# A newly searched order for the first 235 operations of an attention and feed-forward kernel

## The chip, the core and the metric

The kernel runs on one core of a Trainium2 chip. The core has a matrix engine (TensorE, PE in the tables), a vector engine (VectorE, DVE), a scalar engine (ScalarE, ACT), a general engine (GpSimd, POOL) and a queue engine (SyncE, SP) that issues most transfers. Each of them executes its own list of instructions strictly in the order in which the program holds them, and waits at an instruction until what it needs is there. The metric is the device time of one execution in microseconds (us); lower is better.

## The reference, cut to what matters

```python
scores = scale * q_c @ k_c.T                  # 8 x 8 heads, 576 positions in chunks of 64, depth 64
attn = softmax(scores)                        # exp(s - max) / (sum + 1e-9)
x = (attn @ v_c)                              # becomes 4608 rows x 512
h = x @ w_in                                  # 512 x 2048
g = h - tanh(h)
out = g @ w_out                               # 2048 x 512
```

## The kernel before

The 4608 rows are 36 pairs of chunks of 128 rows each, and four pairs make a group of 512 rows; there are nine groups. The first group is the start of the program and is special in two ways. Its weights arrive as 64-bit words and have to be turned into two fp32 halves (high and low) on ScalarE and VectorE first, and its products are fp32 products; the groups after it use fp16 halves. So the first group runs beside the attention of pairs 0 to 7, the loading of all weights and their conversion, and nobody but a hand-searched table, `PLAN`, says in which order this work stands.

`PLAN` is a string of tokens. The program walks through it from left to right and issues the token's instructions, each on the engine that it belongs to; what remains of the order is one list per engine. The tokens that the text below speaks of:

| token | engine | what it does (line) |
|---|---|---|
| `a3`, `v3`, `l1.0`, `l1.1` | SP | load q and k of pair 3; its v; w_in (`.0`) and w_out (`.1`) of block 1 into one of three raw buffers |
| `F9` | PE | nine products of a zero tile `warm`, result in the bank `idle`, read by nobody (L793) |
| `S3`, `T3`, `V3` | PE | scores of pair 3 (L182), its transposed weights (L173), its weighted values (L182) |
| `m3`, `b0`, `r3`, `N3`, `Y3` | DVE | row maximum (L214), subtraction (L219), reciprocals (L240, L241), normalising (L245), low half of x (L275) |
| `E3`, `e0`, `t3`, `X3` | ACT | exponents with the sums in eight parts (L236) or in one (L223), copies out of PSUM (L258), high half of x (L271) |
| `A1`, `H1.0` | ACT | magnitude of weight block 1 (L144), its high half (L159) |
| `s1`, `o1`, `O1`, `L1.0` | DVE | shift (L148), low bits (L152), sign (L156), low half (L163) |
| `G1.1`, `G3` | PE | first feed-forward product of block 1 for rows 256 to 511 (`.0`: rows 0 to 255), of block 3 for all 512 rows (L557) |
| `i1.1`, `k1.1` / `j1.1`, `q1.1` | ACT / DVE | tanh (L568) and high half (L584) / subtraction (L575) and low half (L592) of the same piece |
| `P1.1` | PE | second feed-forward product of that piece (L602) |
| `W1.1` | POOL | a transfer that adds a weight's low half to its high half (L813) |

A product `G` writes a PSUM bank of the pool `ps_h`, which has two. The bank is free for the next product once `j` of the same piece has read it. The zero products write a bank of the same pool, taken once, ahead of the plan:

```python
ps_h = ctx.enter_context(tc.tile_pool(name="ps_h", bufs=2, space=PSUM))
idle = ps_h.tile([P, MOST], F32, name="ph")
    elif kind == "F":
        for _ in range(n):
            nc.tensor.matmul(idle, lhsT=warm[:, :P], rhs=warm, start=True, stop=True)
def gemm1(self, fc, t0, t1):
    ph = ps_h.tile([P, MOST], F32, name="ph")[:, :n]
```

Before, the last `F` token stands ahead of the first `G`, so from the first product on both banks take turns: G1.1, G0.1, G0.0, G3, G1.0 use bank 1, 0, 1, 0, 1 in that order. The attention of pairs 0 to 3 uses two further bank pairs in turn (`two_banks`), where the next pair's step waits until the reader of the pair before is done.

Of the kernel before, what the change touches and what calls it, by code (L numbers as in the profile page):

```python
# [48 lines left out]


PLAN = """
a3 l0.0 a0 a1 l1.0 l1.1 a2 v0 v3 F9 S3 l0.1 l3.0 m3 a5 A0.0 v2 B3 v1 E3 s0.0 l3.1 o0.0 F7 S0 O0.0 a7 m0 H0.0 F3 S1 r3 b0 a4 m1 e0 N3 b1 A1 L0.0 F8 T3 e1 s1 S2 t3 z1 a6 m2 F2 V3 r1 B2 o1 E2 v6 N1 O1 X3 r2 A0.1 l6.0 Y3 l6.1 H1.1 N2 F13 T1 J1.1 s0.1 T2 z0 t1 o0.1 t2 F1 V1 r0 O0.1 V2 X1 v5 N0 H0.1 l8.0 Y1 v4 X2 l8.1 J0.1 L0.1 F4 S5 Y2 H1.0 m5 A3 F1 T0 L1.0 t0 B5 s3 F2 G1.1 E5 o3 V0 O3 G0.1 v7 X0 i1.1 Y0 H3.0 l9.1 S7 l9.0 j1.1 i0.1 L3.0 H3.1 G0.0 k1.1 j0.1 L3.1 k0.1 m7 G3 A6 q0.1 B7 q1.1 i0.0 s6 E7 j0.0 o6 G1.0 L1.1 i3 O6 S6 i1.0 A9 y P1.1 j3 l5.1 l5.0 H6.0 m6 P0.1 H6.1 s9 J6.0 L6.0 k3 B6 o9 G6 W0.6 E6 q3 O9 k0.0 S4 L6.1 J1.0 W0.1 l7.0 l7.1 q0.0 P3 H9.0 m4 H9.1 j1.0 A5 B4 L9.1 L9.0 E4 s5 G9 r7 o5 k1.0 N7 A7 q1.0 O5 T7 i9 P1.0 W1.1 t7 s7 l10.0 H5.1 l10.1 j9 P0.0 W1.0 H5.0 L5.1 k9 L5.0 J5.0 V7 o7 G5 W0.5 X7 q9 O7 A10 r6 l4.1 Y7 P9 l4.0 N6 H7.0 i5 s10 H7.1 L7.0 J5.1 j5 T6 o10 k5 G7 t6 q5 i6 O10 j6 l2.0 H10.1 P5 W1.5 l2.1 L7.1 i7 r5 J10.1 j7 k6 L10.1 A8 q6 V6 N5 k7 P6 s8 H10.0 X6 q7 J10.0 L10.0 Y6 J6.1 W1.6 o8 A2 T5 P7 t5 O8 J3.0 W0.3 s2 H8.0 l15.0 l15.1 H8.1 o2 J8.0 V5 J8.1 G10 L8.0 O2 X5 L8.1 H2.0 l13.0 Y5 l13.1 A4 G8 L2.0 r4 J2.0 s4 i10 N4 J3.1 W1.3 j10 J9.1 W1.9 T4 o4 G2 i8 t4 O4 k10 H2.1 q10 l12.1 H4.1 l12.0 j8 J2.1 V4 L2.1 k8 P10 J4.1 q8 A13 L4.1 i2 s13 H4.0 P8 j2 J7.1 o13 J4.0 J9.0 W0.9 L4.0 O13 k2 G4 A15 q2 l14.0 X4 l14.1 s15 Y4 Wx o15 P2 Z H13.0 i4 L13.0 H13.1 j4 J0.0 W0.0 L13.1 J13.1 G13 O15 k4 A14 q4 l11.1 l11.0 H15.0 s14 H15.1 L15.0 P4 J15.0 L15.1 J15.1 o14 i13 A12 j13 G15 O14 k13 J13.0 s12 H14.0 q13 H14.1 o12 J14.0 P13 J14.1 L14.0 i15 L14.1 J7.0 j15 A11 O12 G14 k15 s11 H12.1 q15 H12.0 L12.1 J12.1 L12.0 P15 J12.0 o11 i14 j14 O11 k14 G12 q14 H11.1 H11.0 L11.1 J11.1 L11.0 J11.0
"""
# [937 lines left out]
```

## Time and profile before

| | us |
|---|---|
| median of three runs (lowest, highest) | 799.54 (799.11, 799.78) |
| the profiled execution | 799.48 |
| its span in the trace | 797.7 |
| TensorE busy in the span | 789.5 (99%) |
| VectorE, ScalarE busy | 628.4 (79%), 496.1 (62%) |
| TensorE busy in the first 10 us, from 10 to 25.3 | 8.49, 13.10 |

The profiled execution lies 0.06 us below the median and 1.8 us above its own span. In the span VectorE is nearly always busy from 10 us on until 77 us (15.16 of 15.30 us between 10 and 25.3), TensorE from 25.3 us on until the end. Rows of the trace read: start, duration, engine, line, operation, output tile <- input tiles, sizes, count, and in brackets how long the engine had been idle and what released it. Consecutive instructions of an engine overlap a little, so the difference between two starts is what an instruction adds to a busy engine.

### The profile page before, as it was taken

The page shows a single profiled execution, that of the slowest core. Times are in us where ns is not written, and L with a number is a line of the kernel's source. Part 1 is how long each engine was busy: PE and PEld are TensorE (multiplying, and loading weights), DVE is VectorE, ACT ScalarE, POOL GpSimd, SP SyncE. Part 2 cuts the span into 40 slices and gives each one's busy share as a digit, 9 for nine tenths or more (in the row PEclk, how much of TensorE's full clock was granted, in tenths as well). Part 3 has the DMA queues.
Part 4 walks back from the last instruction along what each step waited for, and adds up shares of the span by engine and source line. Part 5 has one row for each costly group of instructions (what it writes and reads, how often), then busy time and mean ns, then how long its engine had stood idle before and what let it go on. Part 6 is the DMA issues. An engine that isn't in the chain of part 4 may idle for free.

```text
span 797.7 us, 16317 instructions
## 1 busy us (share of the span) xinstructions
PE 789.5 (99%) x6650; PEld 521.8 (65%) x6650; DVE 628.4 (79%) x1134; ACT 496.1 (62%) x958; POOL 46.5 (6%) x82
## 2 busy tenths in 40 slices
PE   8999999999999999999999999999999999999998
PEld 4777884445676666666666666666666666666664
DVE  7999999999999997868777777777776777655443
ACT  6989968986675656556655555566555655454333
POOL 0022135500000000000000000000000000000000
PEclk9999999999999999999999999999999999999999
DMA  9888848853131223111312231203211220001001
GB/s 359 307 230 227 222 130 177 146 133 80 40 107 40 81 63 110 53 50 46 106 54 53 54 95 50 62 22 97 63 54 42 67 67 15 14 1 53 1 1 54
DMA packets 58731, 72.36 MB, mean 91 GB/s; under 512 B 32800, under 2 KB 33056, under 8 KB 58528
## 3 DMA queue, kind: packets, MB, share of 16 engines
q1 hardware_dynamic: 53760, 61.75, 24.8%
q0 software_dynamic: 4752, 9.44, 6.9%
q8 instruction: 52, 0.85, 0.4%
q14 instruction: 23, 0.19, 0.1%
q10 hardware_dynamic: 144, 0.13, 0.0%
HBM read 45.09 MB, written 9.44 MB: 68 GB/s over the span
## 4 chain that ended last, share of the span: by engine, by line
PE 87%; DVE 8%; ACT 2%; DMA 1%; issue 1%; SPq 0%; DVEq 0%; ACTq 0%
PE po L715 35%; PE ph L657 22%; PE psa L657 9%; PE ph L557 8%; PE po L602 7%; PE psa L423 2%; PE psa L182 2%; DVE w L152 1%; DMA raw<-w_out 1%; PE ps L182 1%; DVE w L156 1%; PE ph L793 1%; DVE wl L163 1%; DMA out<-t 0%; DVE w L148 0%
## 5 line engine op out<-in xcount | busy, mean ns | idle before, releaser
L715 PE MATMUL po<-wl,gh 128*128 128x512 f16 x672 | 154.2, 379 | 0.0
L715 PE MATMUL po<-wl,gl 128*128 128x512 f16 x672 | 154.2, 379 | 0.0
L657 PEld LDWEIGHTS <-wh 128*128 128x128 f16 x1344 | 128.0, 98 | 24.1 <-issue 0.4
L657 PE MATMUL ph<-xh,wl 128*128 128x256 f16 x672 | 114.6, 273 | 0.0
L715 PEld LDWEIGHTS <-gl 128*128 128x128 f16 x672 | 65.8, 98 | 68.0
L715 PEld LDWEIGHTS <-gh 128*128 128x128 f16 x672 | 65.8, 98 | 67.5
L657 PEld LDWEIGHTS <-wl 128*128 128x128 f16 x1008 | 98.6, 98 | 17.2
L657 PE MATMUL ph<-xl,wl 128*128 128x256 f16 x336 | 91.6, 273 | 0.0
L657 PE MATMUL ph<-xh,wh 128*128 128x256 f16 x448 | 76.7, 273 | 0.0
L657 PE MATMUL psa<-xh,wh 128*128 128x256 f16 x448 | 76.4, 273 | 0.3 <-ACT m L649 0.3
L602 PE MATMUL po<-wl,gh 128*128 128x512 f16 (+1 forms) x192 | 63.2, 383 | 0.0
L657 PE MATMUL psa<-xl,wh 128*128 128x256 f16 x224 | 61.1, 273 | 0.0
L657 PE MATMUL ph<-xl,wh 128*128 128x256 f16 x224 | 61.1, 273 | 0.0
L379 ACT ACTIVATE s<-s 128x512 f32<-128x512 f32 x24 | 15.1, 629 | 56.6 <-DVE s L370 56.6
L683 ACT ACTIVATE t<-t,sig 128x512 f32<-128x512 f32 x37 | 26.7, 721 | 35.2 <-DVE t L679 35.0
L683 ACT ACTIVATE t<-wh,sig 128x512 f32<-128x512 f32 x38 | 27.4, 721 | 33.5 <-DVE wh L679 33.3
L683 ACT ACTIVATE t<-spare,sig 128x512 f32<-128x512 f32 x37 | 26.7, 721 | 33.5 <-DVE spare L679 33.5
L557 PE MATMUL ph<-xl,wl 128*128 128x512 f16 x192 | 43.8, 379 | 0.2 <-DVE t L573 0.2
L679 DVE TENSOR_TENSOR t<-ph,t 128x512 f32<-128x512 f32 x28 | 19.2, 686 | 21.9 <-PE ph L657 21.3
L679 DVE TENSOR_TENSOR wh<-ph,wh 128x512 f32<-128x512 f32 x28 | 19.2, 686 | 20.1 <-PE ph L657 19.4
L436 DVE TENSOR_TENSOR xl<-wh,xh 128x512 f16<-128x512 f32 (+1 forms) x56 | 34.3, 615 | 0.4 <-ACT xh L436 0.2
L687 DVE SCALAR_TENSOR_TENSOR wh<-wh,sig,t 128x512 f32<-128x512 f32 x38 | 28.4, 748 | 7.8 <-ACT t L683 7.6
(173 smaller groups left out, 1485.8 us busy)
## 6 DMA issues: line engine op xcount, KB each, us to landing
raw<-w_in SPq DMA_DIRECT2D x16, 512.0 KB, 6.4
raw<-w_out SPq DMA_DIRECT2D x16, 512.0 KB, 6.4
wh<-wl POOLq DMA_DIRECT2D x32, 256.0 KB, 4.2
rawv<-vL SPq DMA_DIRECT2D x28, 256.0 KB, 2.7
rawq<-qL SPq DMA_DIRECT2D x28, 256.0 KB, 3.0
rawk<-kL SPq DMA_DIRECT2D x28, 256.0 KB, 3.2
out<-wh SPq DMA_DIRECT2D x28, 256.0 KB, 2.0
qk<-qkE SPq DMA_DIRECT2D x8, 512.0 KB, 8.7
```

Of the source, the lines that this page charges most:

```text
L152: nc.vector.scalar_tensor_tensor(out=w, in0=low, scalar=29, in1=w, op0=ALU.logical_shift_right, op1=ALU.bitwise_or)
L182: nc.tensor.matmul(ps[os, r, hp * CH:(hp + 1) * CH], lhsT=lhsT(rs, hp, o), rhs=rhs(rs, hp, o), start=True, stop=True)
L379: nc.scalar.activation(s, s, AF.Exp, scale=scale)
L423: nc.tensor.matmul(ps[:, hp, c, :], lhsT=self.v16[p % len(self.v16)][a][:, c, hp, :], rhs=d["a16"][:, b, hp, cs], start=(k == 0), stop=(k ...
L436: return (lambda: nc.scalar.copy(out=h, in_=a)), (lambda: nc.vector.tensor_sub(l, a, h))
L557: nc.tensor.matmul(ph, lhsT=self.weight(fc, 0, a)[:, kc * P:(kc + 1) * P], rhs=x[b][:, kc, cols], start=(k == 0), stop=(k == 3 * KC - 1))
L602: nc.tensor.matmul(self.po[t], lhsT=gg[a][:, ts], rhs=self.weight(fc, 1, b), start=(k == 0), stop=(k == 3 * FC - 1))
L657: nc.tensor.matmul(bank[:, q * 2 * P:(q + 1) * 2 * P], lhsT=self.weight(u, a, i, q, kc), rhs=self.x[j][:, b, kc, :], start=(first and q == ...
L679: nc.vector.tensor_tensor(out=c, in0=self.banks["X"], in1=self.m5 if n % 4 == 3 else c, op=ALU.subtract if n % 4 == 2 else ALU.add)
L683: nc.scalar.activation(t, self.now[n][0], AF.Tanh, scale=self.ff.sig)
L687: nc.vector.scalar_tensor_tensor(out=c, in0=c, scalar=self.ff.sig, in1=t, op0=ALU.mult, op1=ALU.subtract)
L715: nc.tensor.matmul(ff.po[t], lhsT=g[a][:, ts], rhs=half_w[1][fc][:, b], start=(first and s == 0 and k == 0), stop=(last and s == 1 and k = ...
```

## The change

The first 235 tokens of `PLAN` are put into another order; the work in them stays the same, save for the zero products, of which there are 41 in ten tokens instead of 50 in ten. The code is not changed. The two versions agree again from the same token on each engine: TensorE from `P5` on, VectorE from `L7.1` on, apart from a few neighbours that swap places further behind without changing any engine's own list.

```diff
@@ PLAN
-a3 l0.0 a0 a1 l1.0 l1.1 a2 v0 v3 F9 S3 l0.1 l3.0 m3 a5 A0.0 v2 B3 v1 E3 s0.0 l3.1 o0.0 F7 S0 O0.0 a7
+a3 l0.0 a0 a1 a2 l0.1 v2 l1.0 F6 S3 v3 l1.1 m3 a5 A0.0 v1 B3 E3 s0.0 l3.0 l3.1 o0.0 F5 S0 v0 O0.0 m0
...
-X2 l8.1 J0.1 L0.1 F4 S5 Y2 H1.0 m5 A3 F1 T0 L1.0 t0 B5 s3 F2 G1.1 E5 o3 V0 O3 G0.1 v7 X0 i1.1 Y0 H3.0 l9.1 S7 l9.0 j1.1 i0.1 L3.0 H3.1 G0.0
+V2 o1 X1 X2 Y1 A3 Y2 F3 S5 O1 T0 G0.1 t0 m5 l9.0 H1.0 s3 a6 H1.1 V0 v4 L1.0 i0.1 v5 B5 X0 o3 G1.1 l9.1 E5 a4 v7 j0.1 O3 Y0 k0.1 l7.1 F4 S7 H3.0 L1.1 i1.1 G0.0
...
```

The zero products in order: before 9, 7, 3, 8, 2, 13, 1, 4, 1, 2, all ahead of the first `G`; now 6, 5, 3, 1, 3, 3, 11, 3 ahead of the first `G`, then 4 behind `G1.1` and 2 behind `G0.0`. Two places show what moves.

The first place is VectorE from `Y2` on, the last low half of x that the first feed-forward product needs (`xl`), to the first subtraction out of a product's bank (`t<-ph`). In the names the number behind the underscore only tells tiles apart; `wl01` is the low half of block 1's w_in, `w_364` is block 1's words and `w_435`, before `w_492`, block 3's. Before:

```order
L275 TENSOR_TENSOR xl_117<-ps2_433,xh_116 128x4x128
L214 TENSOR_REDUCE mx_489<-ps2_469 128x8
L163 TENSOR_TENSOR wl01_75<-w_291,wh01_74 128x512
L231 TENSOR_SCALAR mx_489<-mx_489 128x8
L148 TENSOR_SCALAR w_492<-w_492 128x1024
L152 SCALAR_TENSOR_TENSOR w_492<-raw_201,w_492 128x1024
L156 SCALAR_TENSOR_TENSOR w_492<-raw_201,w_492 128x1024
L275 TENSOR_TENSOR xl_117<-ps2_529,xh_116 128x4x128
L575 TENSOR_TENSOR t_563<-ph_507,t_563 128x256
```

And the same place now, from `Y2` to `q0.1` (`gl_547`):

```order
L275 TENSOR_TENSOR xl_117<-ps2_414,xh_116 128x4x128
L156 SCALAR_TENSOR_TENSOR w_364<-raw_170,w_364 128x1024
L214 TENSOR_REDUCE mx_480<-ps2_441 128x8
L148 TENSOR_SCALAR w_435<-w_435 128x1024
L163 TENSOR_TENSOR wl01_75<-w_364,wh01_74 128x512
L231 TENSOR_SCALAR mx_480<-mx_480 128x8
L152 SCALAR_TENSOR_TENSOR w_435<-raw_218,w_435 128x1024
L575 TENSOR_TENSOR t_510<-ph_464,t_510 128x256
L156 SCALAR_TENSOR_TENSOR w_435<-raw_218,w_435 128x1024
L275 TENSOR_TENSOR xl_117<-ps2_490,xh_116 128x4x128
L163 TENSOR_TENSOR wl11_77<-w_364,wh11_76 128x512
L592 TENSOR_TENSOR gl_547<-t_510,gh_546 128x256
```

The sign of block 1 (`O1`, L156 on `w_364`) has moved from ahead of `Y2` to behind it; nothing else has crossed `Y2`. The subtraction `j0.1` (L575 on `ph_464`) stands behind `O1`, `m5`, `s3`, `L1.0`, `B5` and `o3`. The next three rows behind `gl_547` are `m7` (L214), `L3.0` (L163) and `j1.1` (L575 on `ph_517`).

The second place is TensorE from the first feed-forward product on, with the waits that the program holds. Before:

```order
L557 MATMUL ph_507<-xh_116,wh01_74 128x256 [waits Activation_49]
L557 MATMUL ph_507<-xh_116,wh01_74 128x256 x3
L557 MATMUL ph_507<-xh_116,wl01_75 128x256 [waits DVE_49]
L557 MATMUL ph_507<-xh_116,wl01_75 128x256 x3
L557 MATMUL ph_507<-xl_117,wh01_74 128x256 x4
L182 MATMUL ps2_529<-aT_501,v_170 64x64 [waits DMAHW7_49,Activation_49]
L182 MATMUL ps2_529<-aT_501,v_170 64x64 x15
L557 MATMUL ph_547<-xh_116,wh00_70 128x256 [waits PE_49]
```

And now, the same engine from `G0.1` (`ph_464`) over `V0` (L182) to `G1.1` (`ph_517`):

```order
L557 MATMUL ph_464<-xh_116,wh00_70 128x256 [waits Activation_49]
L557 MATMUL ph_464<-xh_116,wh00_70 128x256 x3
L557 MATMUL ph_464<-xh_116,wl00_71 128x256 x4
L557 MATMUL ph_464<-xl_117,wh00_70 128x256 x4
L182 MATMUL ps2_490<-aT_477,v_244 64x64 [waits DMAHW6_49,Activation_49]
L182 MATMUL ps2_490<-aT_477,v_244 64x64 x15
L557 MATMUL ph_517<-xh_116,wh01_74 128x256 [waits DVE_49]
```

Behind it stand four zero products, `S7`, then `G0.0` (`ph_576`, which waits for VectorE too), two zero products and `G1.0` (`ph_605`). Since zero products are still to come, the bank `idle` stays taken until the last of them: G0.1, G1.1 and G0.0 all lie in bank 1 of the two now, and G1.0 is the first to get bank 0. The VectorE instruction that `G1.1` waits for is `j0.1`, and the one that `G0.0` waits for is `j1.1`.

More of the change, by code (lines that the diff above doesn't have):

```diff
@@ L51 @@
 PLAN = """
-a3 l0.0 a0 a1 l1.0 l1.1 a2 v0 v3 F9 S3 l0.1 l3.0 m3 a5 A0.0 v2 B3 v1 E3 s0.0 l3.1 o0.0 F7 S0 O0.0 a7 m0 H0.0 F3 S1 r3 b0 a4 m1 e0 N3 b1 A1 L0.0 F8 T3 e1 s1 S2 t3 z1 a6 m2 F2 V3 r1 B2 o1 E2 v6 N1 O1 X3 r2 A0.1 l6.0 Y3 l6.1 H1.1 N2 F13 T1 J1.1 s0.1 T2 z0 t1 o0.1 t2 F1 V1 r0 O0.1 V2 X1 v5 N0 H0.1 l8.0 Y1 v4 X2 l8.1 J0.1 L0.1 F4 S5 Y2 H1.0 m5 A3 F1 T0 L1.0 t0 B5 s3 F2 G1.1 E5 o3 V0 O3 G0.1 v7 X0 i1.1 Y0 H3.0 l9.1 S7 l9.0 j1.1 i0.1 L3.0 H3.1 G0.0 k1.1 j0.1 L3.1 k0.1 m7 G3 A6 q0.1 B7 q1.1 i0.0 s6 E7 j0.0 o6 G1.0 L1.1 i3 O6 S6 i1.0 A9 y P1.1 j3 l5.1 l5.0 H6.0 m6 P0.1 H6.1 s9 J6.0 L6.0 k3 B6 o9 G6 W0.6 E6 q3 O9 k0.0 S4 L6.1 J1.0 W0.1 l7.0 l7.1 q0.0 P3 H9.0 m4 H9.1 j1.0 A5 B4 L9.1 L9.0 E4 s5 G9 r7 o5 k1.0 N7 A7 q1.0 O5 T7 i9 P1.0 W1.1 t7 s7 l10.0 H5.1 l10.1 j9 P0.0 W1.0 H5.0 L5.1 k9 L5.0 J5.0 V7 o7 G5 W0.5 X7 q9 O7 A10 r6 l4.1 Y7 P9 l4.0 N6 H7.0 i5 s10 H7.1 L7.0 J5.1 j5 T6 o10 k5 G7 t6 q5 i6 O10 j6 l2.0 H10.1 P5 W1.5 l2.1 L7.1 i7 r5 J10.1 j7 k6 L10.1 A8 q6 V6 N5 k7 P6 s8 H10.0 X6 q7 J10.0 L10.0 Y6 J6.1 W1.6 o8 A2 T5 P7 t5 O8 J3.0 W0.3 s2 H8.0 l15.0 l15.1 H8.1 o2 J8.0 V5 J8.1 G10 L8.0 O2 X5 L8.1 H2.0 l13.0 Y5 l13.1 A4 G8 L2.0 r4 J2.0 s4 i10 N4 J3.1 W1.3 j10 J9.1 W1.9 T4 o4 G2 i8 t4 O4 k10 H2.1 q10 l12.1 H4.1 l12.0 j8 J2.1 V4 L2.1 k8 P10 J4.1 q8 A13 L4.1 i2 s13 H4.0 P8 j2 J7.1 o13 J4.0 J9.0 W0.9 L4.0 O13 k2 G4 A15 q2 l14.0 X4 l14.1 s15 Y4 Wx o15 P2 Z H13.0 i4 L13.0 H13.1 j4 J0.0 W0.0 L13.1 J13.1 G13 O15 k4 A14 q4 l11.1 l11.0 H15.0 s14 H15.1 L15.0 P4 J15.0 L15.1 J15.1 o14 i13 A12 j13 G15 O14 k13 J13.0 s12 H14.0 q13 H14.1 o12 J14.0 P13 J14.1 L14.0 i15 L14.1 J7.0 j15 A11 O12 G14 k15 s11 H12.1 q15 H12.0 L12.1 J12.1 L12.0 P15 J12.0 o11 i14 j14 O11 k14 G12 q14 H11.1 H11.0 L11.1 J11.1 L11.0 J11.0
@@ new lines @@
+a3 l0.0 a0 a1 a2 l0.1 v2 l1.0 F6 S3 v3 l1.1 m3 a5 A0.0 v1 B3 E3 s0.0 l3.0 l3.1 o0.0 F5 S0 v0 O0.0 m0 F3 S1 r3 b0 m1 e0 F1 S2 N3 H0.0 b1 z0 e1 F3 T3 m2 A0.1 z1 t3 B2 L0.0 F3 V3 E2 s0.1 r1 o0.1 N1 O0.1 X3 r0 H0.1 l6.0 r2 Y3 l6.1 A1 a7 N2 F11 T1 N0 T2 t1 s1 t2 V1 L0.1 V2 o1 X1 X2 Y1 A3 Y2 F3 S5 O1 T0 G0.1 t0 m5 l9.0 H1.0 s3 a6 H1.1 V0 v4 L1.0 i0.1 v5 B5 X0 o3 G1.1 l9.1 E5 a4 v7 j0.1 O3 Y0 k0.1 l7.1 F4 S7 H3.0 L1.1 i1.1 G0.0 q0.1 H3.1 m7 A6 L3.0 j1.1 i0.0 B7 s6 F2 G1.0 E7 j0.0 o6 y P0.1 L3.1 k1.1 S6 O6 i1.0 A9 G3 m6 l5.1 k0.0 H6.1 s9 l5.0 l7.0 B6 q1.1 E6 q0.0 r7 P0.0 o9 L6.1 H6.0 S4 O9 i3 P1.1 L6.0 H9.0 l10.1 j1.0 l10.0 H9.1 m4 G6 k1.0 A5 j3 N7 k3 B4 L9.0 E4 s5 G9 L9.1 o5 A7 q3 T7 q1.0 O5 i9 P3 j9 H5.0 l8.1 s7 l8.0 H5.1 i6 r6 L5.0 P1.0 J1.1 W1.1 o7 J1.0 W0.1 G5 k9 L5.1 t7 O7 A10 q9 l2.1 J5.0 W0.5 V7 j6 v6 H7.0 s10 P9 J0.1 W1.0 L7.0 i5 o10 k6 X7 j5 H7.1 G7 Y7 k5 O10 J5.1 J6.0 W0.6 N6 l4.0 q5 l4.1 T6 i7 l2.0 L7.1 P5 W1.5 H10.1 r5 j7 A8 L10.1 t6 q6 J10.1 N5 V6 k7 s8 P6 H10.0 q7 X6 L10.0 J10.0 Y6 J6.1 W1.6 o8 A2 T5 P7 O8 t5 J3.0 W0.3 s2 l15.0 H8.0 l15.1 H8.1 o2 V5 J8.0 G10 L8.0 J8.1 O2 X5 L8.1 H2.0 l13.0 Y5 l13.1 A4 G8 L2.0 r4 J2.0 s4 i10 N4 J3.1 W1.3 j10 T4 J9.1 W1.9 o4 G2 i8 t4 O4 k10 H2.1 q10 l12.1 H4.1 V4 j8 l12.0 J2.1 P10 L2.1 k8 J4.1 q8 A13 L4.1 P8 i2 s13 H4.0 j2 J7.1 o13 J4.0 J9.0 W0.9 L4.0 O13 k2 G4 A15 q2 l14.0 X4 l14.1 s15 Y4 Wx P2 o15 Z H13.0 i4 L13.0 H13.1 j4 J0.0 W0.0 L13.1 G13 J13.1 O15 k4 A14 q4 l11.1 l11.0 H15.0 s14 P4 H15.1 L15.0 J15.0 L15.1 J15.1 o14 i13 G15 A12 j13 O14 k13 J13.0 s12 H14.0 q13 H14.1 o12 J14.0 P13 J14.1 L14.0 i15 L14.1 J7.0 j15 G14 A11 O12 k15 s11 H12.1 q15 H12.0 L12.1 J12.1 P15 L12.0 J12.0 o11 i14 j14 G12 O11 k14 q14 H11.1 H11.0 L11.1 J11.1 L11.0 J11.0
```

## The prediction

> **What bounds the kernel now.** I read the stretches first, to see which engine is full where, then the chain of waits, then TensorE's own waits, and last the rows around the moved steps. The columns are busy time (and instructions) of PE, PEld, VectorE, ScalarE and GpSimd, then the granted TensorE clock, the transfer engines' share and GB/s.
>
> ```profile
> 0.00:10.00 10.00, 8.49 (x91) 3.71 (x95) 5.44 (x20) 4.82 (x20) 0.20 (x4) 1.00 0.83 314
> 10.00:25.30 15.30, 13.10 (x238) 7.46 (x238) 15.16 (x32) 12.63 (x35) 0.00 (x0) 1.00 1.03 403
> 25.30:62.00 36.70, 36.67 (x330) 30.32 (x329) 36.53 (x62) 32.87 (x111) 5.82 (x9) 1.00 0.80 243
> 62.00:77.30 15.30, 15.30 (x128) 12.05 (x127) 15.20 (x24) 14.39 (x31) 4.34 (x8) 1.00 0.81 228
> 77.30:133.50 56.20, 56.09 (x276) 41.02 (x275) 52.14 (x90) 45.87 (x90) 18.39 (x32) 1.00 0.73 182
> 133.80:797.70 663.90, 659.75 (x5600) 427.28 (x5599) 503.67 (x910) 385.30 (x674) 17.48 (x32) 1.00 0.23 61
> ```
>
> From 10 to 25.3 us VectorE is the full engine (15.16 of 15.30). From 25.3 us on TensorE is, and stays so: 36.67 of 36.70, 15.30 of 15.30, 56.09 of 56.20. TensorE's waits behind 24 us are three:
>
> ```profile
> PE psa L657 <- ACT m L649: 0.3, 1, 0.3
> PE ps L173 <- DVE xl L275: 0.2, 1, 0.2
> PE ph L557 <- DVE t L573: 0.2, 1, 0.2
> ```
>
> The L173 wait lies ahead of the first feed-forward product; the last row is the wait at 133.8 us, where the fp16 groups have begun. So whatever TensorE loses or wins in the changed stretch arrives at the end, less at most the 0.2 us that it waits there for VectorE anyway. The change is to be judged by one question: when has TensorE done the same feed-forward work? The chain of waits shows that work in order (start, us, engine, tile, line):
>
> ```profile
> 24.59 0.66 PE ps L173 x4
> 25.25 0.43 PE ph L793 x2
> 25.68 1.39 PE ph L557 x12
> 27.07 0.62 PE ps L182 x32
> 27.69 1.57 PE ph L557 x12
> 29.27 0.62 PE ps L182 x32
> 29.92 5.81 PE ph L557 x36
> ```
>
> These are T0, the last two zero products, G1.1, V0, G0.1, S7, then G0.0, G3 and G1.0. At 29.92 us T0, G1.1, G0.1, V0 and S7 are done; the new order has done the same five when it reaches G0.0, since all the attention products ahead of T0 are the same ones. My measure is therefore the start of G0.0, before 29.92 us.
>
> **The change part by part.** First, six zero products instead of nine ahead of S3.
>
> ```profile
> qk<-qkE SPq DMA_DIRECT2D x1, 512.0 KB, 3.7
> 0.74 0.40 SPq L198 DMA_DIRECT2D qk<-qkE  x1
> 1.19 4.02 PE L793 MATMUL ph<-warm 128*128 128x512 bf16 x9 [1.19 <-DVE col L758]
> 5.14 1.13 PE L182 MATMUL ps<-qk 64*64 64x64 f32 x32
> 15.11 2.98 PE L793 MATMUL ph<-warm 128*128 128x512 bf16 x13
> 7.34 2.49 ACT s L236 x16
> 9.85 0.18 DVE sm L240
> 28.18 0.63 ACT L271 CAST xh<-ps 128x512 fp32r<-128x512 f32 x1
> 29.49 0.39 ACT L568 ACTIVATE t<-ph 128x256 f32<-128x256 f32 x1
> ```
>
> The first transfer is issued at 0.74 us and lands 3.7 us later, at 4.44; the scores start at 5.14. They waited for the zero products, not for the data (the wait is booked on the transfer, but landing is 0.7 us older). Nine products take 4.02 us, 0.45 each; six end at 3.9 us. S3 then starts at about 4.5, 0.64 us sooner. Behind it stand m3, then E3 (2.49 us on ScalarE), and the reciprocals r3 at 9.85 us wait for E3: that chain moves along. S0, which VectorE also needs ahead of r3, comes behind five zero products: S3 ends at 5.6; five products are 1.1 us at 0.23 each (2.98/13) and 2.2 at 0.45; S0 at the 1.13 us of a slow S3 ends by 8.9 at worst, so m0 (0.6 us) ends at 9.5 where r3 could start at 9.2. The gain is 0.3 to 0.64 us; I take 0.6, the end that follows if the products behind 6 us run at the later rate.
>
> Second, O1 leaves the stretch ahead of Y2. From 10 us on VectorE has no gap, so Y2 moves by what O1 adds there:
>
> ```profile
> 24.46 0.68 DVE L214 TENSOR_REDUCE mx<-ps 128x8 f32<-128x512 f32 x1
> 25.05 0.68 DVE L163 TENSOR_TENSOR wl<-w,wh 128x512 fp32r<-128x512 f32 x1
> 25.65 0.16 DVE L231 TENSOR_SCALAR mx<-mx 128x8 f32<-128x8 f32 x1
> 25.73 0.68 DVE L148 TENSOR_SCALAR w<-w 128x1024 uint32<-128x1024 uint32 x1
> 26.45 1.23 DVE L152 SCALAR_TENSOR_TENSOR w<-raw,w 128x1024 uint32<-128x1024 uint32 x1
> 27.71 1.23 DVE L156 SCALAR_TENSOR_TENSOR w<-raw,w 128x1024 uint32<-128x1024 uint32 x1
> 28.85 0.68 DVE L275 TENSOR_TENSOR xl<-ps,xh 128x512 fp32r<-128x512 f32 x1
> 29.45 0.41 DVE L575 TENSOR_TENSOR t<-ph,t 128x256 f32<-128x256 f32 x1
> 29.78 0.68 DVE L163 TENSOR_TENSOR wl<-w,wh 128x512 fp32r<-128x512 f32 x1
> ```
>
> By the differences of starts: a maximum 0.59, a low half 0.60, B 0.08, s 0.72, o 1.26, O 1.14, Y 0.60, a half-size j 0.33 (0.41 to its end). O1 is an O: Y2 moves up by 1.14 + 0.6 = 1.74 us. VectorE is free behind Y2 at 24.46 - 1.74 = 22.72, and T0 starts at 24.59 - 1.74 = 22.85.
>
> Third, the bank. TensorE: T0 0.66, G0.1 1.57, V0 0.62, done at 25.7. G1.1 needs the bank of G0.1, so it waits for j0.1. VectorE from 22.72: O1 1.14, m5 0.59, s3 0.72, L1.0 0.60, B5 0.08, o3 1.26, j0.1 to its end 0.41, sum 4.80: 27.5. ScalarE has the tanh i0.1 ready by then: its queue ahead of it holds only t0 and two high halves. G1.1 starts at 27.6; TensorE stood idle for 1.9 us. Behind G1.1 (1.57) come four zero products (0.92) and S7 (0.62): 30.7. VectorE has meanwhile done O3 1.14, Y0 0.60, L1.1 0.60 and q0.1 0.33 (30.1) and waits for S7, because m7 stands ahead of j1.1: m7 0.59, L3.0 0.60, j1.1 0.41 from 30.75 end at 32.35. G0.0 waits for j1.1 and starts at 32.4, after a second idle 1.7 us. That is 2.5 us later than 29.92. Queued behind the waiting G1.1 are S7 and through it E7, s6 and o6; none of them is waited for sooner than TensorE gets there.
>
> Fourth, two zero products behind G0.0, 2 x 0.23 = 0.46 us, on TensorE's path with nothing to cover them: 2.96 us. G1.0 gets the other bank and waits for TensorE alone. Behind it P0.1, S6 and G3 find their inputs. G0.0 ends at 34.0; its tanh (0.39) and E7 (2.49) end near 36.9 us; j0.0 0.33, o6 1.14 and L3.1 0.60 end near 36.6; TensorE wants them at 37.4 and 38.0. From G6 on the banks alternate again. VectorE has waited 0.6 us for S7 and some 1.4 for the tanh of G0.0 by then, so it runs closer to TensorE than before; I bound further waits by 0 and 0.6 us and take 0, the nearest row being 36.67 of 36.70 busy.
>
> Fifth, what I cost at nothing. The transfers are the same ones; w_out of block 1 falls from sixth to tenth place. At 403 GB/s a 512 KB load is 1.3 us, so it lands near 14.9 us, and A1 wants it at 17 or later; if that cover were gone A1 would delay s1 and Y2 by the same. GpSimd's first adds come in another order, W1.1 first instead of W0.6, and start some 12 us later:
>
> ```profile
> 64.63 0.86 POOL L813 DMA_DIRECT2D wh<-wl  x1 [6.88 <-ACT gh L584]
> ```
>
> Before, the queue then idles 6.88 us ahead of W1.5, which waits for work that is later now too; a rest of up to 3 us would hit only later adds, the first readers of which come behind 115 us.
>
> The sum: -1.74 (T0 earlier), -0.43 (two zero products gone ahead of G1.1), +1.9 and +1.7 (two waits for the bank), +1.38 (six zero products among the real ones), +0.15 of rounding and of G halves (1.39 to 1.57) comes to +2.96. Less the 0.2 us wait at 133.8 us that TensorE no longer has: +2.75. Against the profiled execution, 799.48 us (span 797.7, 0.06 below the median), that is 802.2 us.
>
> The Trainium skill, Perfetto Trace Analysis, section Optimizing Tensor Performance, says that independent groups of products should rotate through different PSUM banks, so that reading one out overlaps the next. In the rows above the read-out costs nothing as long as two banks alternate. By the page the change should cost the read-out time between G0.1 and G1.1 and again ahead of G0.0; it gives no figure.
>
> **The rivals.** *No real wait for the bank.* Should G1.1 and G0.0 not wait for j, G1.1 would start with L1.0 at 25.9, S7 would follow E5 (V0 at 25.7, a copy of 0.63 and E5 of 2.49: 28.8) and end at 29.4, and G0.0 would start there: 0.5 us earlier than before, and the two zero products take 0.46 back. That gives 799.4, no change. For it speaks only the table's own order, where G1.1 stands ahead of j0.1; against it the wait that the program holds.
>
> *Faster.* The advance of Y2 would come through whole: 1.74 + 0.43 = 2.17 us, 797.3, if the zero products behind G1.1 and G0.0 only filled waits and j0.1 came before V0's end. It decides at j0.1: VectorE would have to end it by 25.7 instead of 27.5. It has 4.80 us queued behind Y2 and only 2.9 us for it. Waits and zero products together under 0.6 us would make it faster.
>
> *TensorE slow for longer.* The granted clock reads 1.00 throughout, yet the first nine zero products take 0.45 each and the thirteen later 0.23, and the first scores 1.13 us. If with six products, a gap of 0.6 us and S3 the slow rate held until S1, then S0 would end at 8.9, three products at 10.2 and S1 at 11.3, so m1 would start near 11.3 instead of 10.1: 1.2 us more, 803.4 us. The Trainium skill, TensorE: Matmul & The Clock Gate, Part 1, has the array at half rate until a window of about 3.4 us was busy, and back there after as long an idle one. By that rule the waits of 1.9 and 1.7 us would not slow it again; no run here has shown an idle stretch of that length.
>
> **How the numbers follow.** The forecast has 0.62: its own range is 801.2 (the bank waits 1 us shorter, since VectorE's column of 4.8 us is the longest guess) to 803.1 (gain of 0.3 instead of 0.6 at S3, and 0.6 more behind G6). The slow TensorE has 0.12, no wait for the bank 0.16, faster 0.10. About 0.2%, 1.6 us, is what a measurement of this kernel can tell from no change, so slower by more begins at 801.1. Slower is 0.75, the same 0.15, faster 0.10. A range that leaves out the faster case (0.10), the part of the second that ends below 799.5 (0.07) and the third's far end (0.03) reaches from 799.5 to 803.7.
>
> **What would show it.** Right: S3 at about 4.5 us; T0 near 22.9; TensorE idle for about 1.9 us ahead of G1.1 and 1.7 ahead of G0.0, both released by VectorE at L575, G0.0 near 32.4; a full TensorE behind; the wait at 133.8 us gone or put down to a TensorE that is 2.7 us late. Wrong: S3 still at 5.1; no release by L575; products at 0.45 us behind 7 us; or TensorE's lateness at G0.0 absorbed before 133 us, which would need idle time that the rows before do not show.

## The result, and the profile after

| | before | after |
|---|---|---|
| median of six runs each, us (lowest, highest) | 799.49 (799.11, 799.78) | 805.72 (804.34, 807.46) |
| ratio of the two, with its 95% interval | | 1.0079 (1.0069 to 1.0089) |
| the profiled execution, us | 799.48 | 806.50 |
| its span, us | 797.7 | 804.7 |

The change makes the kernel 6.2 us slower; the forecast was 2.7. The stretches of the changed kernel, with the columns and windows of the prediction:

```profile
0.00:10.00 10.00, 7.13 (x110) 3.33 (x111) 6.51 (x23) 4.74 (x20) 0.20 (x4) 1.00 0.81 309
10.00:25.30 15.30, 12.31 (x235) 8.25 (x238) 15.20 (x31) 12.61 (x33) 0.00 (x0) 1.00 0.94 357
25.30:62.00 36.70, 33.46 (x273) 26.22 (x275) 32.58 (x56) 30.02 (x104) 1.93 (x3) 0.95 0.63 219
62.00:77.30 15.30, 15.30 (x129) 12.15 (x128) 13.75 (x20) 12.50 (x28) 7.78 (x10) 1.00 0.90 221
77.30:133.50 56.20, 54.04 (x263) 41.07 (x263) 50.92 (x90) 45.73 (x94) 18.24 (x29) 1.00 0.75 184
```

TensorE was full from 25.3 us on before. Now it misses 3.2 us between 25.3 and 62 us, at a clock of 0.95, and another 2.2 us between 77.3 and 133.5 us. The first hole in TensorE's own rows, from T0 to the product behind the last two zero products:

```profile
22.49 0.66 PE L173 MATMUL ps<-ident,s 128*128 128x128 f32 x4
...
26.94 0.74 PE L557 MATMUL ph<-xh,wh 128*128 128x256 f32 x4 [1.36 <-DVE t L575]
...
31.84 0.93 PE L557 MATMUL ph<-xh,wh 128*128 128x256 f32 x4 [1.75 <-DVE t L575]
32.57 1.06 PE L557 MATMUL ph<-xh,wl 128*128 128x256 f32 x4
33.42 1.05 PE L557 MATMUL ph<-xl,wh 128*128 128x256 f32 x4
34.28 1.08 PE L793 MATMUL ph<-warm 128*128 128x512 bf16 x2
35.42 0.81 PE L557 MATMUL ph<-xh,wh 128*128 128x256 f32 x4
36.06 0.62 PE L557 MATMUL ph<-xh,wl 128*128 128x256 f32 x4
```

The two bracketed rows are G1.1 and G0.0, both released by the subtraction L575. Behind the second wait four products `ph<-xh,wl` take 1.06 us, where they take 0.62 from 36.06 us on, and the granted clock (the last column but two) says why:

```profile
30.00:32.00 2.00, 0.25 (x9) 0.16 (x2) 1.84 (x5) 1.22 (x2) 0.00 (x0) 1.00 1.02 405
32.00:33.00 1.00, 1.00 (x7) 1.00 (x7) 0.46 (x1) 0.00 (x0) 0.00 (x0) 0.61 1.06 420
33.00:34.00 1.00, 1.00 (x6) 1.00 (x6) 0.00 (x0) 0.00 (x0) 0.00 (x0) 0.50 0.65 258
34.00:35.00 1.00, 1.00 (x5) 0.36 (x3) 0.07 (x1) 0.48 (x3) 0.00 (x0) 0.50 0.12 49
```

The second hole lies elsewhere. These are TensorE's waits in it, the first of them at 105.88 us, all ahead of second feed-forward products (L602) for their input (us in total, times, longest):

```profile
PE po L602 <- DVE gl L592: 1.3, 2, 0.8
PE po L602 <- ACT gh L584: 0.9, 1, 0.9
```

They come behind a late load. The chain of waits passes through a late load of w_out in both kernels; before, it stood there as 87.38 with 5.59 us. The changed kernel's:

```profile
92.17 8.01 DMA raw<-w_out
```

ScalarE's magnitude `A` (L144) of that load and of the one ahead of it is my measure of it. First the two rows of before, then those of after:

```profile
86.28 1.16 ACT L144 ACTIVATE w<-raw 128x1024 f32<-128x1024 f32 x1
93.06 1.13 ACT L144 ACTIVATE w<-raw 128x1024 f32<-128x1024 f32 x1 [0.38 <-DMA raw<-w_out]
```

```profile
91.07 1.15 ACT L144 ACTIVATE w<-raw 128x1024 f32<-128x1024 f32 x1
100.28 1.13 ACT L144 ACTIVATE w<-raw 128x1024 f32<-128x1024 f32 x1 [3.39 <-DMA raw<-w_out]
```

The first of the two comes 4.8 us late; from it to the next takes 9.21 us instead of 6.78. I call this the load stretch. ScalarE's lateness is thus 4.8 us by 91 us and 7.2 at 100 us (TensorE's own was 4.2 at T4, which starts at 81.32 instead of 77.11 us); 7.0 reach the end. Beside the load run GpSimd's adds, before and after:

```profile
86.16 0.86 POOL L813 DMA_DIRECT2D wh<-wl  x1 [3.72 <-ACT junk L167]
89.06 0.86 POOL L813 DMA_DIRECT2D xh<-xl  x1 [2.00 <-DVE xl L275]
91.71 0.86 POOL L813 DMA_DIRECT2D wh<-wl  x1 [1.15 <-ACT junk L167]
```

```profile
88.25 0.70 POOL L813 DMA_DIRECT2D wh<-wl  x1
92.56 0.86 POOL L813 DMA_DIRECT2D wh<-wl  x1 [0.18 <-issue]
93.85 0.86 POOL L813 DMA_DIRECT2D xh<-xl  x1 [0.28 <-DVE xl L275]
```

Before, GpSimd waits for data ahead of each of these adds: its queue is empty. After, the brackets are nearly gone: it issues as soon as the add two places earlier has landed (this is waited for by a small copy, `tick`, L812; these waits rise from 28.3 to 41.7 us in all), since the first add comes at 56.5 us instead of 42.7.

So there are three suspects: the held bank, the slow clock, and the adds beside the load.

### The profile page after: what moved, and what is told of

It is laid out like the page before. It is cut to its first block, busy times and chain, and to the rows that moved or that the text cites. A ratio compares the mean times of both kernels' runs of the same rounds, so it can differ in the third digit from the quotient of the medians.

```text
span 804.7 us, 16298 instructions
## 1 busy us (share of the span) xinstructions
PE 789.2 (98%) x6636; PEld 521.4 (65%) x6641; DVE 628.8 (78%) x1134; ACT 496.0 (62%) x958; POOL 49.3 (6%) x82
## 4 chain that ended last, share of the span: by engine, by line
PE 84%; DVE 10%; DMA 3%; ACT 2%; issue 1%; SPq 0%; DVEq 0%; ACTq 0%
PE po L715 35%; PE ph L657 22%; PE psa L657 9%; PE ph L557 6%; PE po L602 6%; PE psa L423 2%; PE psa L182 2%; DMA raw<-w_in 2%; DVE w L152 1%; DVE w L156 1%; DMA raw<-w_out 1%; DVE wl L163 1%; DVE w L148 1%; DVE t L575 1%; ACT w L144 1%
## 5 line engine op out<-in xcount | busy, mean ns | idle before, releaser
L602 PE MATMUL po<-wl,gh 128*128 128x512 f16 (+1 forms) x192 | 63.2, 383 | 0.0
```

The source lines that it names most:

```text
L602: nc.tensor.matmul(self.po[t], lhsT=gg[a][:, ts], rhs=self.weight(fc, 1, b), start=(k == 0), stop=(k == 3 * FC - 1))
```

## The experiments

### The bank and the clock

First, the zero products write a bank of the second feed-forward product (`po`), which is free until later; nothing else is changed.

```diff
-idle = ps_h.tile([P, MOST], F32, name="ph")
+idle = ff.po[1]
```

> The changed order, with the zero products writing the bank of the second output tile (which no real product uses before P0.0) instead of a bank of the products' pool. Theory A (the held bank is the first cause, and the late weight stream behind 60 us follows from it): no L575 wait ahead of G1.1 and G0.0, full clock, G0.0 starts near 29.0 us (31.8 in the changed kernel, 29.9 before), end 798.5 to 799.8 us. Theory B (a second cause of its own: GpSimd's adds, some 13 us later, collide with the weight loads): the same start of G0.0, but TensorE waits again near 105 us, end 800.5 to 802.5. Rival (the bank is not the cause): G0.0 stays near 31.8, end 805 or more.

Measured 801.93 us (ratio 1.0033, 1.0019 to 1.0048): 3.8 us of the 6.2 are gone. That is theory B's time, not A's, yet TensorE does not wait near 105 us in this profile. L575 is left with one wait of 0.2 us. The profiled execution also met a late v3:

```profile
16.18 1.13 PE L182 MATMUL ps<-aT,v 64*64 64x64 f32 x32 [2.54 <-DMA v<-vE]
```

Behind that wait the clock fell to 0.50 for over three microseconds too (its mean from 17 to 20 us is 0.58), and T0 came at 24.75.

Second, the same in the other direction: the kernel before, with one zero product behind G0.0, which is enough to hold the bank.

```diff
-H3.1 G0.0 k1.1
+H3.1 G0.0 F1 k1.1
```

> The kernel before with one zero product more, put behind G0.0 (token F1): nothing else moves, but the zero products' bank is now held until there, so G1.1, G0.1 and G0.0 share one bank. Theory A: G0.1 waits for j1.1 and G0.0 for j0.1, G0.0 starts near 32.4 us (29.9 before) and the end is 801.8 to 803.2, up to 804.5 if the granted clock drops in the wait as it did in the changed kernel. Rival (a bank held costs nothing in this order): 799.7, the 0.23 us of one zero product.

Measured 803.76 us (1.0053, 1.0038 to 1.0068). One product of 0.4 us costs 4.5. In its rows G0.1 now waits, and the clock falls:

```profile
29.91 0.72 PE L557 MATMUL ph<-xh,wh 128*128 128x256 f32 x4 [2.20 <-DVE t L575]
```

```profile
30.00:32.00 2.00, 2.00 (x12) 1.94 (x12) 0.45 (x1) 0.00 (x0) 0.00 (x0) 0.66 1.03 376
32.00:34.00 2.00, 2.00 (x37) 1.72 (x36) 1.23 (x3) 1.58 (x5) 0.00 (x0) 0.50 0.81 322
```

Third, to part the wait from the clock: the same kernel, with eight zero products into the `po` bank ahead of G0.1, so that TensorE stays busy while it waits.

```diff
-G0.1
+U8 G0.1
+elif kind == "U":
+    for _ in range(n):
+        nc.tensor.matmul(ff.po[1], lhsT=warm[:, :P], rhs=warm, start=True, stop=True)
```

> The kernel before with the bank held by one zero product behind G0.0, as in the run before, and eight zero products in the output tile's bank between V0 and G0.1, where TensorE waited 2.2 us: the wait stays, but TensorE is busy in it. Theory (the clock drops because of the idle stretch, and cost about 1.7 of the 4.5 us): granted clock 1.00 throughout, G0.0 near 31.6 us instead of 33.2, end 801.8 to 802.6. Rival (the clock drops for another reason, or the slow stretch is hidden): 803.5 to 804.

Measured 803.19 us (1.0047, 1.0032 to 1.0062). The clock reads 1.00 throughout, and behind it stands G0.0:

```profile
30.00:32.00 2.00, 2.00 (x40) 1.87 (x44) 0.53 (x1) 0.34 (x2) 0.00 (x0) 1.00 1.04 395
```

```profile
32.56 0.74 PE L557 MATMUL ph<-xh,wh 128*128 128x256 f32 x4 [0.31 <-DVE t L575]
```

So it was the idle time that took the clock down. But the full clock brings only 0.6 us here, less than expected, and the runs of the two kernels overlap (802.8 to 804.05 and 802.57 to 803.38, four each). G0.0 comes at 32.56 instead of 33.23, against 29.92 before, and ScalarE's tanh at 75 us is still 3.9 us late. Most of the cost is the wait itself. TensorE is 2.6 us late at G0.0, 3.2 at the next product G3, behind the added zero product (34.59 instead of 31.40), and 3.5 at T4 (80.62 instead of 77.11); the last 0.3 us of this, and the 0.4 us by which ScalarE is later still, I did not locate.

### What an own bank leaves

With the bank out of the way, the new order should have been faster than before by its earlier T0. It is not. One suspect was the late v3. In the next kernel v3 is loaded ahead of v2:

```diff
 idle = ff.po[1]
-l0.1 v2 l1.0 F6 S3 v3 l1.1
+l0.1 v3 l1.0 F6 S3 v2 l1.1
```

> The changed order with the zero products in the output tile's bank, as in the run with the own bank, and one more edit: the loads of v2 and v3 change places, so that v3, which V3 needs near 13 us, is the seventh load again instead of the ninth. Theory C (the 2.7 us that the own bank left over come from the early wait for v3 and the clock that drops in it): V3 starts near 13 us, T0 near 22.5, G0.0 near 29.0, full clock throughout, end 798.3 to 799.6 and a spread under 2 us. Rival (the rest is the late weight stream, or zero products among the real ones): 801 to 802.5 as with the own bank alone.

Measured 801.13 us (1.0026, 1.0011 to 1.0042): the rival's time. It is 0.8 us less than without the swap, which lies inside the spread of both. T0 came at 22.94 at full clock, yet the tanh at 75 us at 75.32 (before 75.21). And the load stretch is long again:

```profile
86.76 1.14 ACT L144 ACTIVATE w<-raw 128x1024 f32<-128x1024 f32 x1
95.84 1.12 ACT L144 ACTIVATE w<-raw 128x1024 f32<-128x1024 f32 x1 [2.73 <-DMA raw<-w_out]
```

So in this profile T0's lead is gone by 75 us without any bank wait, and the loss at the end comes with a load stretch of 9.08 us. The next kernel frees the bank otherwise: the six late zero products are left out, and the banks alternate as before.

```diff
-G1.1 l9.1 E5 ... F4 S7 ... F2 G1.0
+G1.1 l9.1 E5 ... S7 ... G1.0
-v2 l1.0 F6 S3 v3
+v3 l1.0 F6 S3 v2
```

> The changed order without the four zero products behind G1.1 and the two behind G0.0 (so the last zero product stands ahead of the first G, and the two banks take turns from there), and with v2 and v3 changed about. Theory A with C: no L575 wait ahead of G1.1 or G0.0, G0.0 near 29.0, G1.0 0.5 us sooner than with the own bank, end 797.8 to 799.2. Rival: the missing zero products let the clock drop between G1.1 and S7, end 800 to 801.5.

Measured 801.41 us (1.0032, 1.0015 to 1.0049), no better: S7 and G0.0 now wait where the zero products stood (1.50 us for ScalarE, 0.51 for VectorE), and the load stretch is 8.34 us. The time is the rival's, but not by its cause: the clock reads 1.00 throughout the changed stretch. Where T0's lead goes can be read from TensorE's busy time up to 25 and 36 us, all products first and then the zero products alone. The kernel before:

```profile
0.00:25.00 25.00, 21.29 (x320) 1.00 0.95 367
0.00:36.00 36.00, 32.27 (x467) 1.00 0.91 351
...
0.00:25.00 25.00, 14.10 (x48) 1.00 0.95 367
0.00:36.00 36.00, 14.69 (x50) 1.00 0.91 351
```

The new order with the own bank and the swapped loads:

```profile
0.00:25.00 25.00, 19.53 (x323) 1.00 0.87 337
0.00:36.00 36.00, 29.91 (x466) 1.00 0.86 329
...
0.00:25.00 25.00, 10.26 (x35) 1.00 0.87 337
0.00:36.00 36.00, 11.91 (x41) 1.00 0.86 329
```

By 25 us real products have 7.19 us before and 9.27 now, a lead of 2.08. By 36 us they have 17.58 and 18.00: 0.42 are left. In between the new order spends 1.65 us on six zero products (before 0.59 on two) and 0.62 on a wait for ScalarE. What TensorE has next is not ready sooner: VectorE, which was busy for 20.30 of the first 25 us before, was so for 20.81 here, a lead of 0.5 us and not of 2.08. An earlier T0 alone was tried on the kernel before:

```diff
-F9 S3
+F6 S3
```

> The kernel before with six zero products instead of nine ahead of the first scores, and nothing else. By the prediction's first step S3 starts at 4.4 to 4.6 us (5.1 before), VectorE's full stretch and T0 0.6 to 0.9 us sooner, and TensorE, full from there, ends 0.5 to 0.9 us sooner: 798.4 to 798.8. Rival (the clock stays low for longer, or the next transfers are then late): 799.2 to 800.

Measured 799.17 us (1.0000, 0.9991 to 1.0009). T0 came 0.85 us sooner, at 23.74, and the profiled execution ended 0.66 us sooner; over ten runs nothing is left of it that could be told from none.

### The adds beside the load

The kernel before, with its first five adds all issued late (W0.5 first, the other four right behind it; in the changed kernel W1.1 and W0.1 come ahead of W0.5):

```diff
-W0.6 ... W0.1 ... W1.1 ... W1.0 ... W0.5
+W0.5 W1.1 W0.1 W1.0 W0.6
```

> The kernel before with the first five adds in the order W0.5, W1.1, W0.1, W1.0, W0.6, all behind G5: the first starts near 55.3 us instead of 42.7, and nothing else moves. Theory B: the adds meet the weight loads between 52 and 75 us, the loads land later, TensorE waits ahead of 133 us, end 800.8 to 802.5. Theory A: 799.2 to 800.0.

Measured 799.35 us (1.0003, 0.9994 to 1.0013), load stretch 6.92 us: late first adds alone do nothing there, although they make the later ones bunch up as well (issued at 76.24, 79.20, 82.55, 86.10, 88.75 and 90.83 us, none of them after a wait for data of more than 0.3 us). The changed kernel, with three of the splits `J` (sums of squares on ScalarE, L167, which an add waits for) and the adds behind them moved back early, to about where they stood before:

```diff
-o7 J1.0 W0.1 ... J0.1 W1.0 ... J6.0 W0.6
+A6 J1.0 J0.1 ... G1.0 W0.1 ... P0.0 W1.0 H6.0 J6.0 ... G6 W0.6
```

> The changed order with GpSimd's first five adds as early as their last readers allow: J1.0, J0.1 and J6.0 (the sums of squares, ScalarE) moved ahead, adds in the order W0.1, W1.0, W0.6, W1.1, W0.5. The first add starts near 37 us instead of 56.5. Theory B: the loads behind 60 us land 1 to 3 us sooner, TensorE's waits of 0.9 and 0.85 us near 105 us shrink or go, end 802.5 to 804.3. Theory A: the same waits, end 805 to 806.5.

Measured 805.63 us (1.0086, 1.0055 to 1.0117), which is no gain by the median. Its profile has the load stretch at 6.68 us (92.62 to 99.30) as expected, but stands 1.5 us later than the changed kernel at its start (92.62 against 91.07): the clock averages 0.80 between 23 and 40 us, against 0.90 there. Next, the changed kernel without four of the adds; four weight parts then lack their low halves from there on.

```diff
-add(h, l)
+if (part, fc) not in {(0, 3), (1, 3), (1, 9), (0, 9)}:
+    add(h, l)
```

> The changed kernel without the four GpSimd adds that run between 82 and 93 us (W0.3, W1.3, W1.9, W0.9), so that these four weight parts go on without their low halves; all else as changed. Theory (the adds slow the w_out load): the stretch from the conversion at 91 us to the next falls from 9.2 us to 6.5 to 7.2, the one megabyte add of x starts some 7 us earlier, and the end comes 1.8 to 2.6 us earlier, at 803.1 to 803.9 us. Rival (the load's own place among the loads): the stretch stays over 8.5 us and the end at 805.0 to 806.5. Rival (the add of x alone does it, and now it starts earlier): the stretch at 91 us falls but an earlier one grows by as much, the end at 805 or later.

Measured 804.61 us (1.0068, 1.0049 to 1.0088; runs from 801.8 to 808.2). The stretch:

```profile
94.61 1.15 ACT L144 ACTIVATE w<-raw 128x1024 f32<-128x1024 f32 x1
101.41 1.13 ACT L144 ACTIVATE w<-raw 128x1024 f32<-128x1024 f32 x1 [0.94 <-DMA raw<-w_out]
```

6.80 us as before the change: in the changed kernel these adds lengthened it. The median missed its range. The profiled execution, the longest of the six at 808.19 us, was 8.3 us late by 94 us, with a wait of 2.4 us for v3 and a clock of 0.83 between 10 and 20 us and 0.80 between 23 and 40. With the bank free the early adds were tried twice more, on the two kernels above:

```diff
 idle = ff.po[1]              # or: no F4, no F2
-l0.1 v2 l1.0 F6 S3 v3 l1.1
+l0.1 v3 l1.0 F6 S3 v2 l1.1
-o7 J1.0 W0.1 ... J0.1 W1.0 ... J6.0 W0.6
+A6 J1.0 J0.1 ... G1.0 W0.1 ... P0.0 W1.0 H6.0 J6.0 ... G6 W0.6
```

> The new order with the zero products in a bank of their own, v3 loaded before v2, and the splits of two groups of w_out and one of a later group (J1.0, J0.1, J6.0) and five GpSimd adds moved back to about where they stood before. Theory (the adds come 14 us later and run close behind one another until 97 us, so they share the transfer engines with the w_out load of 88 us): the stretch between that load's conversion and the one before it falls from 9.1 us to 6.6 to 7.2, and the end comes at 798.3 to 799.6 us. Rival (that load is late by the order of the loads themselves, not by the adds): the stretch stays at 8.3 to 9.2 us and the end at 801. Rival (the moved splits delay the tanh around 75 us by as much as the adds give): tanh at 76 to 77 us and the end at 800 to 801.

> The new order without the six zero products behind the first one (the four ahead of S7 and the two ahead of the product of o6 and G1.0), v3 loaded before v2, and the same splits and adds moved back as in the one with a bank of their own. Theory: as there, the stretch ahead of the late w_out conversion at 6.6 to 7.2 us (8.3 without the early adds) and the end at 798.3 to 799.8 us; rival: 801 as without them.

Measured 801.73 us (1.0038, 1.0026 to 1.0050) and 801.08 us (1.0028, 1.0016 to 1.0040). The stretch fell from 9.08 to 8.15 us and from 8.34 to 7.03, and the tanh at 75 us went from 75.32 to 77.31 and from 76.07 to 76.45: near the last rival of the first expectation. How much of that the moved splits cost is not shown, for 1.0 of the first kernel's 2.0 us is there ahead of all of them: T0 comes at 23.96 instead of 22.94. In that execution TensorE was slow for longer at the start, as one rival of the prediction had it, although the granted clock reads 1.00 (five zero products, then S0; the changed kernel took 1.25 and 0.69 us for them):

```profile
5.66 2.32 PE L793 MATMUL po<-warm 128*128 128x512 bf16 x5
7.91 1.14 PE L182 MATMUL ps<-qk 64*64 64x64 f32 x32
```

The four later adds beside the load were next moved without the splits, to behind the clearing of v16 (L297) in GpSimd's queue:

```diff
 idle = ff.po[1]              # v2 and v3 swapped as above
-add(h, l)
+if (part, fc) in {(0, 3), (1, 3), (1, 9), (0, 9)}:
+    held.append((h, l))
+else:
+    add(h, l)
 att, half = Late(late), Half(late)
+for h, l in held:
+    add(h, l)
```

> The zero products in a bank of their own, v3 loaded before v2, and the four GpSimd adds W0.3, W1.3, W1.9 and W0.9 issued behind the clearing of v16 at 104 us, so that only the add of x runs beside the late w_out load, as before; nothing is left out. Theory (of the changed kernel's 6.2 us the held bank with its slow clock and the early loads are some 4, and the bunched adds the other 2.4): the stretch from the conversion at 87 us to the next falls from 9.1 us to 6.6 to 7.2, and the end comes at 798.8 to 799.9 us, level with before: the new order itself brings nothing, since TensorE's lead of 2.1 us of products at 25 us goes into zero products and waits until 36 us. Rival (the four adds now hold up GpSimd's reductions at 117 us or the loads of the second group): the end at 800.5 to 802 us, with a reduction waiting for a tick. Rival (something else of the new order costs 2 us): the stretch stays over 8 us, the end at 801.

Measured 799.81 us (1.0011, 1.0002 to 1.0020), in the range. The stretch (one line lower in this kernel) is 6.85 us:

```profile
86.35 1.15 ACT L145 ACTIVATE w<-raw 128x1024 f32<-128x1024 f32 x1
93.20 1.14 ACT L145 ACTIVATE w<-raw 128x1024 f32<-128x1024 f32 x1 [0.43 <-DMA raw<-w_out]
```

A reduction on GpSimd (L115) came late behind the fourth of the adds, at 117.31 us instead of 113.73. Two last kernels put the four adds right behind that of x, once with the own bank and once in the changed kernel as it is:

```diff
-W1.6 ... W0.3 ... W1.3 ... W1.9 ... W0.9 ... Wx ... W0.0
+W1.6 ... Wx ... W0.0 W0.3 W1.3 W1.9 W0.9
```

> The zero products in a bank of their own, v3 loaded before v2, and the four adds W0.3, W1.3, W1.9, W0.9 right behind those of x and W0.0 in GpSimd's queue (before the clearing of v16), so that they land by 105 us and GpSimd is free for its reductions at 113 us. The add of x waits for the last low half of x at about 89 us, which empties the queue ahead of the late w_out load. Theory: the stretch ahead of that load's conversion at 6.7 to 7.2 us as with the adds behind the clearing, the reductions end at 117 us or sooner instead of 118.7, and the end comes 0.4 to 0.9 us sooner than there: 798.9 to 799.5 us, level with before. Rival (the reductions were not what the last 0.4 us went into): 799.8 us again. Rival (the four adds now slow the loads behind 93 us): the last low half of w_out behind 111 us and the end at 800.5 or more.

> The changed kernel with the same four adds behind those of x and W0.0, the zero products still in the bank of the feed-forward pool. Theory (two separate losses that add up): the stretch ahead of the late w_out conversion falls from 9.2 us to 6.7 to 7.2, the two waits of TensorE for the bank and the slow clock behind them stay, and the end comes at 803.0 to 804.3 us, that is 3.5 to 5 us above the kernel with a bank of its own. Rival (the held bank pushes everything late, and the adds bunch up only because of it): 805 us or more, with the stretch at 9 us. Rival (the bank matters little once the adds are out of the way): under 801.5 us.

With the own bank: 799.67 us (1.0004, 0.9995 to 1.0013), which cannot be told from before. Stretch 6.94 us:

```profile
87.00 1.15 ACT L144 ACTIVATE w<-raw 128x1024 f32<-128x1024 f32 x1
93.94 1.12 ACT L144 ACTIVATE w<-raw 128x1024 f32<-128x1024 f32 x1 [0.54 <-DMA raw<-w_out]
```

Its last reduction still ends at 118.4 us, so the 0.1 us to the kernel ahead of it says nothing of the reductions. In the changed kernel: 805.24 us (1.0072, 1.0051 to 1.0092; runs from 802.2 to 807.7), above the range expected, though the stretch there is 5.94 us. In its profile both waits for the bank are followed by a slow clock, where in the changed kernel only the second was.

```profile
27.17 1.05 PE L557 MATMUL ph<-xh,wh 128*128 128x256 f32 x4 [1.48 <-DVE t L575]
...
33.68 0.80 PE L557 MATMUL ph<-xh,wh 128*128 128x256 f32 x4 [1.75 <-DVE t L575]
```

```profile
28.00:30.00 2.00, 1.93 (x10) 1.81 (x10) 1.78 (x4) 1.55 (x9) 0.00 (x0) 0.50 1.03 321
...
34.00:36.00 2.00, 2.00 (x13) 1.91 (x11) 0.29 (x1) 0.00 (x0) 0.00 (x0) 0.55 0.23 90
```

Adds beside the load do not always lengthen it. With the own bank and nothing else changed, an add (issued at 89.28 us) and that of x (92.07) ran beside that load (89.47 to 95.26), yet the stretch is 6.97 us:

```profile
88.39 1.16 ACT L144 ACTIVATE w<-raw 128x1024 f32<-128x1024 f32 x1
95.36 1.12 ACT L144 ACTIVATE w<-raw 128x1024 f32<-128x1024 f32 x1 [0.56 <-DMA raw<-w_out]
```

That profile lost its time earlier: T4 comes at 79.23 us there, before at 77.11. Why an overlap lengthens the load in one kernel and not in another stays open.

## Why the prediction was right and wrong

The direction and the main cause held; the time lay 3.5 us below the result and the range ended 2 us below it. By its steps:

- *Six zero products ahead of S3*: right. S3 was forecast at 4.5 us and came at 4.40; T0 at 22.85, and came at 22.49.
- *The measure at G0.0*: right. Forecast 32.4 us, measured 31.84, with waits of 1.36 and 1.75 us (forecast 1.9 and 1.7), both on L575. That the bank is the first cause was shown from both sides: an own bank takes 3.8 us away, one zero product on the kernel before adds 4.5. The rule cited there (the Trainium skill, Perfetto Trace Analysis, section Optimizing Tensor Performance) agrees: once the banks no longer alternate, the read-out, with VectorE's queue ahead of it, stands between two products, and TensorE waits 1.36 and 1.75 us.
- *Two zero products behind G0.0, 0.46 us*: mis-sized. G0.0 and the two took from 31.84 to 35.42, 3.58 us for some 2.0, with the clock at 0.50 for most of it. The prediction left it at full speed because the waits are short. It had cited the Trainium skill, TensorE: Matmul & The Clock Gate, Part 1: half rate comes after an idle window of about 3.4 us. Here half rate came behind 1.75 and 2.20 us of idle; the measurement decides. The rival of a slow TensorE was thought of for the first ten microseconds alone. There it did not come true in the changed kernel's profile (zero products at 0.25 us each from 5.24 us on), but it did in another execution, above.
- *The step that failed most is the fifth part, "what I cost at nothing".* It followed the adds to their next reader behind 115 us and asked only whether they come too late. It did not ask what runs beside them on the way. The adds bunch up, and a w_out load's stretch grows by 2.4 us (9.21 against 6.78); without four of them, or with these four moved, it is 6.80 and 5.94. TensorE, which the prediction had full to the end, waits 2.2 us behind it. That they share the transfer engines with the load is the likely link, but no run shows it by itself. The row it quoted, GpSimd's idle 6.88 us ahead of W1.5, is no safeguard: on the kernel before, late first adds closed that gap, and the time stayed (799.35).
- *"Whatever TensorE wins or loses in the changed stretch arrives at the end"*: half right. Losses arrived. The gain at T0, forecast at 1.74 us, did not: with an own bank and the v3 swap the same order is level at 75 us, since its lead of products at 25 us goes into more zero products (1.06 us) and a wait for ScalarE (0.62). The sum sets zero products and waits against this gain, so up to G0.0 it lost nothing by it. A better mark than TensorE's place at T4 is the last weight conversion, the last L144 (at 102.67 us before): in all profiles here the end is as late as this mark to within 1 us. The changed kernel has 7.2 us there and 7.0 at the end; own bank and v3 swap 2.75 and 2.1, when TensorE was only 0.4 us late at T4.

The terms can be laid beside four profiled executions of the new order with a held bank: how far the execution lies above the 799.48 us of before, less the excess of the load stretch over 6.78 us, less the time lost to the clock (17 us between 23 and 40 us times one less its mean clock; in one kernel 1.7 us more between 10 and 20).

| kernel | above before | load | clock | rest |
|---|---|---|---|---|
| changed | 7.0 | 2.4 | 1.7 | 2.9 |
| changed, early adds | 5.6 | -0.1 | 3.4 | 2.3 |
| changed, four adds less | 8.7 | 0.0 | 5.1 | 3.6 |
| changed, adds behind x | 5.0 | -0.8 | 3.4 | 2.4 |

The rest lies about the 2.75 us that the prediction gave to the bank and the zero products. This table is arithmetic, not a test: where the clock was set right by itself, on the kernel before with a held bank, its 1.7 us were worth only 0.6 at the end, so part of the slow clock is waited for anyway. What runs show is this: own bank, v3 swap and moved adds together bring 805.72 us back to 799.67, level with before. The own bank alone brings 3.8 us, with the v3 swap 4.6; bank and swap bring 5.6 where the adds are moved (805.24 to 799.67). The adds bring 1.5 us by the medians where the bank is free (801.13 to 799.67; the intervals of the two ratios just overlap), and where it is held 0.5 us (805.72 to 805.24), which runs that lie 5.5 us apart don't let one tell from nothing.

The record has more on the held bank than these medians: the mean granted clock of every run. One fall to 0.50 for some 3.4 us takes about 0.002 off it (1.7 of 800 us).

| kernel | runs at a mean clock of 0.999 or 1.000, us | runs at 0.993 to 0.998, us |
|---|---|---|
| changed | 804.34, 805.15 | 805.52 to 807.46 |
| changed, early adds | 803.55 | 805.07 to 809.00 |
| changed, four adds less | 801.78, 802.97 | 804.02 to 808.19 |
| changed, adds behind x | 802.19, 802.44 | 804.47 to 807.71 |

In each of the four the runs that by this mean had no fall are the shortest. Against the median of before in its own round, these lie 5.3 us higher in the changed kernel, 3.5 without the four adds and 2.9 with the adds behind x. So at full clock the four adds cost 1.8 to 2.3 us there, near the 2.4 us of the load stretch; 2.9 us are left for the bank and the zero products, to which the prediction gave 2.75; and the last 1.0 us of the changed kernel's median goes with the clock. These are two runs each, sorted after the fact: a strong hint, not a test. Nor is it all of the spread: the longest run without the six late zero products, 806.30 us, has a mean clock of 1.000. What sets that one stays open.
